# Attention into a squared-ReLU layer: decoding float64 weights with an integer addition of the low word

## The chip, the cores and the metric

The kernel runs on one core of a Trainium2 chip. The metric is device time in microseconds (us), the median of several runs. PE is the matrix engine, DVE the vector engine, ACT the scalar engine (ScalarE), POOL GpSimd, SP the engine that only issues DMAs here. Each engine works through its own list of instructions in order and waits there for what it needs.

## The reference

Eight batches of eight heads, 576 tokens, 64 dimensions a head. Keys and values are first pooled into 32 memory slots by a softmax over tokens (`phi`), then the queries attend to those slots, and the result, as 4608 rows of 512, goes through two weight matrices with a squared ReLU between them.

```python
a = softmax(phi, over tokens)                 # 576 x 32 per head
k_m = einsum('bhsm,bhsd->bhmd', a, k)
v_m = einsum('bhsm,bhsd->bhmd', a, v)
attn = softmax(q @ k_m.T / 8)                 # 576 x 32
x = (attn @ v_m) as (4608, 512)
out = (relu(x @ w_in) ** 2) @ w_out           # w_in 512 x 2048, w_out 2048 x 512
```

`w_in` and `w_out` arrive as float64, everything else as float32.

## The kernel before, in words

Weights are kept as pairs of float32r numbers, a high part and the rest, and each product of two such pairs is made of three matmuls (`hi*hi`, `hi*lo`, `lo*hi`). `v_m @ w_in` is formed first (`vw`), so that the layer's input matrix is small; `mm1` multiplies it with the attention weights (`ath`, `atl`), ScalarE and DVE square the positive part (`r`, `gh`, `glo`), and `mm2` multiplies with `w_out` (`wo`) into four accumulators.

Work runs in this order: the memory slots and attention of batch 0 (`memory`, `scores`, `attention`), then eight steps over slices of `w_in` and blocks of `w_out`, in which weights are decoded just ahead of their first use, batch 1 between them, then pairs of batches with all weights present (`w_out` in SBUF, the decoded `w_in` stored to DRAM in two tensors and read back).

`decode` turns one 128 x 512 piece of float64 into the pair; there are 16 pieces of `w_in` and 16 of `w_out`. A float64 is two 32-bit words: `high` (sign, exponent, 20 bits of mantissa) and `low` (32 bits). They alternate in the buffer `raw`, so that each is read with a step of two words. `work` holds two halves, `T` and `W`. The steps, with lines of the profile:

- L322 (DVE) clamps `high`, read as a float32, to what float32 can hold; L323 (ACT) scales it, which moves the exponent to float32's bias.
- L324 (DVE) takes the sign bit, L325 (DVE) shifts the scaled word left by 3 and joins the sign: `W` now is the weight as float32 with 3 bits of mantissa still zero.
- L326 (DVE) masks `W` down to sign and exponent, a power of two; L327 (DVE) multiplies `low` by 2^-52 and by that power: the value that the low word is worth.
- L330 (DVE) adds the two floats. For the 14 pieces of `w_out` after the first block this addition is left out; a DMA from POOL's queue (L343) adds the value into the lower part of the pair later.
- L338 copies the high part (ACT or DVE, the compiler's helper line is L260), L339 (DVE) subtracts it to get the rest. For `w_in` two DMAs from POOL's queue (L346) store the pair to DRAM.

The kernel records every operation first, with a cost and a latency, and a list planner (`Plan.order`) sets the order in which they are issued; operations that may run on two engines are given to one there. Raw loads, decode and the preparation of later batches are marked as leading work. The framework below may order instructions anew within an engine. So a change of one step's cost moves other steps.

Of the kernel before, what the change touches and what calls it, by code (L numbers as in the profile page):

```python
# [14 lines left out]
AF = mybir.ActivationFunctionType  # L15
ALU = mybir.AluOpType
# [3 lines left out]
P = 128  # L20
EPS = 1e-9
SIGN = 0x80000000
POWER = 0xFF800000
TOP = struct.unpack("<f", struct.pack("<I", 0x47EFFFFF))[0]

STEP = 5200
# [26 lines left out]
class Plan:  # L53
# [21 lines left out]
    def op(self, ways, fn, r=(), w=(), lead=False, cap=None, port=None, size=0, lat=120):  # L75
        o = Op()
        o.ways, o.fn, o.lead, o.cap, o.port, o.size, o.lat = ways, fn, lead, cap, port or {}, size, lat
        deps = set()
        for accesses, writing in ((r, False), (w, True)):
            for a in accesses:  # L80
                b, key = a if isinstance(a, tuple) else (a, None)
                assert not b.closed, b.slot
                if b.before is not None:
                    deps.update(b.before.users)
                for k, ops in b.written.items():
                    if key is None or k is None or k == key:
                        deps.update(ops)
                if writing:
                    for k, ops in b.read.items():
                        if key is None or k is None or k == key:  # L90
                            deps.update(ops)
        for accesses, writing in ((r, False), (w, True)):
            for a in accesses:
                b, key = a if isinstance(a, tuple) else (a, None)
                b.users.append(o)
                if writing:
                    if key is None:
                        b.written, b.read = {None: [o]}, {}
                    else:
                        b.written[key] = [o]  # L100
                        b.read.pop(key, None)
                else:
                    b.read.setdefault(key, []).append(o)
        deps.discard(o)
        o.deps, o.users, o.seq = deps, [], len(self.ops)
        for d in deps:
            d.users.append(o)
        self.ops.append(o)
        return o
# [77 lines left out]
def tt(n):  # L187
    return 150 + 1.04 * n


def ts(n):
    return 150 + 0.52 * n


def act(n):
    return 120 + 0.86 * n
# [10 lines left out]
def tile_attention_moe(  # L207
# [20 lines left out]
    nc = tc.nc  # L228
# [15 lines left out]
    ND = 512  # L244
# [5 lines left out]
    op = plan.op  # L250
    ENG = {"DVE": nc.vector, "POOL": nc.gpsimd, "ACT": nc.scalar}

    def st(shape, dt, tag, name, n=1):
        return plan.buf(tag, lambda slot: sb.tile(shape, dt, tag=slot, name=name, bufs=1), n)
# [4 lines left out]
    def copy(e, o, i):  # L259
        nc.scalar.copy(o, i) if e == "ACT" else ENG[e].tensor_copy(o, i)  # L260

    def dma(fn, size, r=(), w=(), eng="SP", two=False, **more):
        e = {"SP": nc.sync, "POOL": nc.gpsimd}[eng]
        issue = 700 if eng == "POOL" else 1250 if two else 620
        return op({eng: issue}, lambda _: fn(e.dma_start), r=r, w=w, size=size, lat=0, **more)

    def vec(ways, fn, r, w, port=BOTH, **more):
        return op(ways, fn, r=r, w=w, port=port, **more)
# [30 lines left out]
    wo = {}  # L299

    def wi_rows(x, s, hh):

        return w_in_parts[x]()[2 * hh * P:(2 * hh + 2) * P, s * SL:(s + 1) * SL].rearrange("(c p) f -> p c f", p=P)

    def decode(kind, j, h, room):

        rb, wb = (st([P, 2 * ND], U32, tag, name, 2 if tag == "KV" else 1) for tag, name in zip(room, ("raw", "work")))
        if kind == "wi":
            src = w_in_u[:, 2 * h:2 * h + 2, j * SL:(j + 1) * SL, :]
        else:  # L310
            src = w_out_u[:, 2 * j + h:2 * j + h + 1]
        R = rb
        T = lambda: wb()[:, 0:ND]
        W = lambda: wb()[:, ND:2 * ND]
        low = lambda: R().rearrange("p (n t) -> p n t", t=2)[:, :, 0]
        high = lambda: R().rearrange("p (n t) -> p n t", t=2)[:, :, 1]
        tf = lambda: T().bitcast(F32)
        wf = lambda: W().bitcast(F32)
        rk, tk, wk = (rb, "r"), (wb, "t"), (wb, "w")
        dma(lambda d: d(R().rearrange("p (c f t) -> p c f t", c=src.shape[1], t=2), src), 4096 * P, w=[rk], lead=True)  # L320

        vec({"DVE": ts(ND)}, lambda e: nc.vector.tensor_scalar(tf(), high().bitcast(F32), TOP, -TOP, ALU.min, ALU.max), [rk], [tk], lead=True)  # L322
        op({"ACT": act(ND)}, lambda e: nc.scalar.activation(tf(), tf(), AF.Copy, scale=2.0 ** -112), [tk], [tk], lead=True)  # L323
        vec({"DVE": ts(ND)}, lambda e: nc.vector.tensor_scalar(W(), high(), SIGN, None, ALU.bitwise_and), [rk], [wk], lead=True)  # L324
        vec({"DVE": tt(ND)}, lambda e: nc.vector.scalar_tensor_tensor(W(), T(), 3, W(), ALU.logical_shift_left, ALU.bitwise_or), [tk, wk], [wk], lead=True)  # L325
        vec({"DVE": ts(ND)}, lambda e: nc.vector.tensor_scalar(T(), W(), POWER, None, ALU.bitwise_and), [wk], [tk], lead=True)  # L326
        vec({"DVE": tt(ND)}, lambda e: nc.vector.scalar_tensor_tensor(tf(), low(), 2.0 ** -52, tf(), ALU.mult, ALU.mult), [rk, tk], [tk], lead=True)  # L327
        late = kind == "wo" and j > 0
        if not late:
            vec({"DVE": tt(ND)}, lambda e: nc.vector.tensor_add(wf(), wf(), tf()), [tk, wk], [wk], lead=True)  # L330
        if kind == "wi":
            t = wi[0, j, 0, h] = st([P, 2, 2, SL], F32R, "wi", f"wi0_{j}_{h}", 3)
            part = lambda x: t()[:, x].rearrange("p c f -> p (c f)")
        else:
            t = wo[2 * j + h] = st([P, 2, DM], F32R, f"W{j}{'ab'[h]}", f"wo{j}{h}")
            part = lambda x: t()[:, x]
        k0, k1 = ((t, (h, x) if kind == "wi" else x) for x in (0, 1))
        op({"ACT": act(ND), "DVE": ts(ND)}, lambda e: copy(e, part(0), wf()), [wk], [k0], lead=True, port={"DVE": True})  # L338
        vec({"DVE": tt(ND)}, lambda e: nc.vector.tensor_sub(part(1), wf(), part(0).bitcast(F32)),  # L339
            [wk, k0], [k1], lead=True)  # L340
        if late:

            dma(lambda d: d(out=part(1), in_=tf(), accum_op=ALU.add), 4096 * P, [tk, k1], [k1], eng="POOL", lead=True)  # L343
        if kind == "wi":
            for x in (0, 1):
                dma(lambda d, x=x: d(wi_rows(x, j, h), t()[:, x].bitcast(F32)), 2048 * P, r=[(t, (h, x))], w=[(w_in_parts[x], (j, h))], eng="POOL", lead=True)  # L346
# [230 lines left out]
    part = {}  # L577
# [128 lines left out]
    def piece(kind, j):  # L706
        raws, works = (x.split() for x in free[j if j > 3 else 0])
        for h in (0, 1):
            t = turn[0]
            turn[0] += 1  # L710
            decode(kind, j, h, (raws[t % len(raws)], works[t % len(works)]))
# [82 lines left out]
```

## Time and profile before

| | |
|---|---|
| time, median of 3 runs | 836.11 us (831.14 to 837.33) |
| span of the profiled execution | 831.4 us; its own time is not given apart |
| PE busy | 763.5 us (92%) |
| DVE busy | 571.2 us (69%) |
| ACT busy | 378.1 us (45%) |
| DMA | 101.56 MB, mean 122 GB/s |

A busy share is a mean over very different stretches: DVE is near full while weights are decoded and half idle later. The page's lists of waits and the chain of waits tell which engine another one stood still for. The span is the time from the first to the last instruction.

### The profile page before, as it was taken

The numbers are of one execution on the slowest core, as the hardware profiler recorded it, in microseconds if no ns is written. First come the engines' busy times: TensorE is split into PE (matmuls) and PEld (weight loads), VectorE is DVE, ScalarE is ACT, GpSimd is POOL, SyncE is SP. The second block draws the span as 40 slices with busy tenths as digits, with TensorE's granted clock in tenths as the row PEclk, the third lists the DMA queues.
The fourth block names the chain that finished last, engine by engine and source line by source line (L and its number), as shares of the span: only waits on it lengthen the run. The fifth ranks groups of instructions, "written<-read, shape, count | busy, mean of one in ns | idle before, by whom it ended". The sixth has DMA issues, their size and how long they took to land.

```text
span 831.4 us, 12939 instructions
## 1 busy us (share of the span) xinstructions
PE 763.5 (92%) x4756; PEld 643.3 (77%) x4756; DVE 571.2 (69%) x1266; ACT 378.1 (45%) x871; POOL 67.4 (8%) x105
## 2 busy tenths in 40 slices
PE   3468789989989899999999999999999999999995
PEld 2245578878768688888888888888788888888884
DVE  3899899898446756696768465786768556774540
ACT  1235466656535245563436355463435355552320
POOL 3113112222100100001000100000000100000000
PEclk9959999999999899999999999999999999999998
DMA  7947966657665443322552533323422433100001
GB/s 210 302 153 223 261 192 203 178 174 212 159 161 151 116 132 102 102 80 52 143 142 72 135 111 99 117 54 81 140 61 69 138 93 99 53 16 36 1 1 63
DMA packets 93091, 101.56 MB, mean 122 GB/s; under 512 B 24868, under 2 KB 78116, under 8 KB 93028
## 3 DMA queue, kind: packets, MB, share of 16 engines
q1 hardware_dynamic: 80292, 81.55, 33.2%
q0 software_dynamic: 12736, 19.19, 9.5%
q8 instruction: 37, 0.61, 0.3%
q14 instruction: 26, 0.21, 0.1%
HBM read 79.17 MB, written 17.83 MB: 117 GB/s over the span
## 4 chain that ended last, share of the span: by engine, by line
PE 73%; issue 10%; DVE 8%; DMA 3%; ACT 2%; POOL 2%; SPq 0%; POOLq 0%; DVEq 0%; ACTq 0%
PE h L603 20%; PE acc L636 12%; PE acc L633 12%; PE acc L634 12%; PE accl L659 4%; PE pvw L494 4%; PE psc L532 3%; PE pkv L408 3%; DMA q<-in_q_dram 2%; PE pvw L475 1%; DVE vw L503 1%; DVE qT L527 1%; ACT vw L260 1%; DMA wo<-work 1%; DVE work L325 1%
## 5 line engine op out<-in xcount | busy, mean ns | idle before, releaser
L603 PE MATMUL h<-ath,vw 128*128 128x320 f32 (+1 forms) x1024 | 213.9, 300 | 8.9 <-ACT ath L260 6.3
L633 PE MATMUL acc<-wo,gh 128*128 128x512 f32 x512 | 207.0, 404 | 2.7 <-ACT gh L609 2.5
L634 PE MATMUL acc<-wo,gh 128*128 128x512 f32 x512 | 201.7, 394 | 0.0
L603 PEld LDWEIGHTS h<-ath,vw 128*128 128x128 f32 x1024 | 172.5, 190 | 25.7 <-ACT ath L260 6.7
L636 PE MATMUL acc<-wo,glo 128*128 128x512 f32 x512 | 161.5, 409 | 3.0 <-DVE glo L613 2.8
L503 DVE TENSOR_TENSOR vw<-pvw,vw 64x256 fp32r<-64x256 f32 x192 | 78.5, 420 | 68.0 <-ACT vw L260 66.2
L633 PEld LDWEIGHTS acc<-wo,gh 128*128 128x128 f32 x512 | 97.1, 190 | 23.3 <-ACT gh L609 3.8
L260 ACT CAST vw<-pvw 64x256 fp32r<-64x256 f32 (+1 forms) x206 | 74.9, 381 | 83.9 <-PE pvw L494 37.6
L603 PE MATMUL h<-atl,vw 128*128 128x256 f32 (+1 forms) x512 | 110.5, 297 | 0.0
L634 PEld LDWEIGHTS acc<-wo,gh 128*128 128x128 f32 x512 | 96.9, 189 | 16.9
L636 PEld LDWEIGHTS acc<-wo,glo 128*128 128x128 f32 x512 | 90.5, 191 | 21.4 <-DVE glo L613 7.6
L609 ACT ACTIVATE gh<-r 128x512 fp32r<-128x512 f32 x128 | 80.7, 631 | 45.3 <-DVE r L608 38.5
L613 DVE TENSOR_TENSOR glo<-r,gh 128x512 fp32r<-128x512 f32 x128 | 87.6, 684 | 5.1 <-ACT r L611 2.9
L608 DVE TENSOR_SCALAR r<-h 128x256 f32<-128x256 f32 (+1 forms) x109 | 49.7, 458 | 59.0 <-PE h L603 58.1
L607 ACT ACTIVATE r<-h 128x256 f32<-128x256 f32 (+1 forms) x147 | 58.8, 407 | 67.8 <-PE h L603 59.8
L603 PEld LDWEIGHTS h<-atl,vw 128*128 128x128 f32 x512 | 83.0, 190 | 0.5 <-DVE atl L570 0.2
L611 ACT ACTIVATE r<-r 128x576 f32<-128x576 f32 x93 | 63.7, 685 | 2.1
L610 ACT ACTIVATE gl<-r 128x64 fp32r<-128x64 f32 x128 | 32.7, 256 | 63.2 <-DVE r L608 61.0
L659 PE MATMUL accl<-wo,gl 128*128 128x512 f32 x192 | 53.0, 400 | 0.1
L532 PE MATMUL psc<-qT,kb 128*128 128x256 f32 (+1 forms) x128 | 43.3, 465 | 5.8 <-DVE S L536 3.1
L494 PE MATMUL pvw<-wi,VTh 128*128 128x256 f32 x192 | 38.1, 290 | 3.8 <-DVE vw L503 3.7
L659 PEld LDWEIGHTS accl<-wo,gl 128*128 128x128 f32 x192 | 35.4, 191 | 7.3 <-DVE o L260 0.5
(94 smaller groups left out, 818.5 us busy)
## 6 DMA issues: line engine op xcount, KB each, us to landing
wi<-w_in_hi SPq DMA_DIRECT2D x56, 256.0 KB
wi<-w_in_lo SPq DMA_DIRECT2D x56, 256.0 KB
q<-in_q_dram SPq DMA_DIRECT2D x32, 288.0 KB
KV<-in_k_dram SPq DMA_DIRECT2D x32, 256.0 KB
KV<-in_v_dram SPq DMA_DIRECT2D x32, 256.0 KB
raw<-in_moe_w_in_dram SPq DMA_DIRECT2D x16, 512.0 KB
raw<-in_moe_w_out_dram SPq DMA_DIRECT2D x16, 512.0 KB
out_dram<-o POOLq DMA_DIRECT2D x20, 256.0 KB, 8.4
```

What stands on the lines that cost most here:

```text
L260: nc.scalar.copy(o, i) if e == "ACT" else ENG[e].tensor_copy(o, i)
L494: nc.tensor.matmul(pw()[:, x * SL:(x + 1) * SL], l()[:, 2 * hh + x, :], w(r, x), start=(i == 0), stop=(i == 2))
L503: vec({"DVE": tt(SL)}, lambda e, V=V, pr=pr, src=src: nc.vector.tensor_sub(V()[pr, 1, hh, :], src(), V()[pr, 0, hh, :].bitcast(F32)), [pw, ...
L532: nc.tensor.matmul(pq()[:, 0:32 * n], kb()[:, x].rearrange("p h m -> p (h m)"), qT()[:, x, 0:n].rearrange("p c t -> p (c t)"), start=(x == ...
L603: nc.tensor.matmul(p()[:, 0:n], V()[:, l, hh, c0:c0 + P], x()[:, hh, cs], start=(i == 0), stop=(i == 5))
L609: op({"ACT": act(SM)}, lambda e: nc.scalar.activation(gh(), r()[:, 0:SM], AF.Square), [r], [gh])
L611: op({"ACT": act(S), **({} if b < 2 else {"DVE": tt(S)})}, lambda e: nc.scalar.activation(r(), r(), AF.Square) if e == "ACT" else nc.vecto ...
L613: vec({"DVE": tt(SM)}, lambda e: nc.vector.tensor_sub(glo(), r()[:, 0:SM], gh().bitcast(F32)), [r, gh], [glo])
L633: nc.tensor.matmul(a(), gh()[:, c], t()[:, 0], start=f0, stop=False)
L634: nc.tensor.matmul(a(), gh()[:, c], t()[:, 1], start=False, stop=False)
L636: nc.tensor.matmul(a(), glo()[:, c], t()[:, 0], start=False, stop=f1)
L659: nc.tensor.matmul(a(), G()[:, l, :], t()[:, w], start=(ff == 0 and n == 0), stop=(ff == NFF - 1 and n == 2))
```

## The change

The low word is no longer turned into a float. ScalarE multiplies it by 2^-29 and writes it back as a rounded integer (0 to 8) in its place in `raw`; one integer addition on DVE puts it into the three free bits of `W`, with carry. The mask, the product and the float addition go, and so do the 14 accumulating DMAs, for `w_out` pieces are now complete like those of `w_in`.

```diff
-POWER = 0xFF800000
...
         vec({"DVE": tt(ND)}, lambda e: nc.vector.scalar_tensor_tensor(W(), T(), 3, W(), ALU.logical_shift_left, ALU.bitwise_or), [tk, wk], [wk], lead=True)
-        vec({"DVE": ts(ND)}, lambda e: nc.vector.tensor_scalar(T(), W(), POWER, None, ALU.bitwise_and), [wk], [tk], lead=True)
-        vec({"DVE": tt(ND)}, lambda e: nc.vector.scalar_tensor_tensor(tf(), low(), 2.0 ** -52, tf(), ALU.mult, ALU.mult), [rk, tk], [tk], lead=True)
-        late = kind == "wo" and j > 0
-        if not late:
-            vec({"DVE": tt(ND)}, lambda e: nc.vector.tensor_add(wf(), wf(), tf()), [tk, wk], [wk], lead=True)
+        op({"ACT": act(ND)}, lambda e: nc.scalar.activation(low(), low(), AF.Copy, scale=2.0 ** -29), [rk], [rk], lead=True)
+        vec({"DVE": tt(ND)}, lambda e: nc.vector.tensor_tensor(W(), W(), low(), ALU.add), [rk, wk], [wk], lead=True)
...
-        if late:
-
-            dma(lambda d: d(out=part(1), in_=tf(), accum_op=ALU.add), 4096 * P, [tk, k1], [k1], eng="POOL", lead=True)
```

In the changed kernel lines stand one lower up to the new ScalarE line (L325) and the integer addition (L326), and seven lower behind `decode`: the clamp is L321, ACT's scaling L322, the sign L323, the shift L324, the subtraction L335.

The order of the built programs, at three places. First DVE, up to the transpose `at_1_0` of batch 0 (L566, then L559), from the sum `rz_1` of the second head group on. Before:

```order
L397 TENSOR_TENSOR phi_0_170<-phi_0_170,pmx_0_399 128x640
L548 TENSOR_REDUCE rz_1_None<-S_1_384 128x18
L326 TENSOR_SCALAR work<-work 128x512
L549 TENSOR_SCALAR rz_1_None<-rz_1_None 128x18
L322 TENSOR_SCALAR work<-raw 128x512
L550 RECIPROCAL rz_1_None<-rz_1_None 128x18
L327 SCALAR_TENSOR_TENSOR work<-raw,work 128x512
L551 TENSOR_TENSOR S_1_384<-S_1_384,rz_1_None 128x576
L330 TENSOR_TENSOR work<-work 128x512
L566 STREAM_TRANSPOSE at_1_0_445<-S_1_384 128x256
```

Now:

```order
L541 TENSOR_REDUCE rz_1_None<-S_1_409 128x18
L476 TENSOR_TENSOR vw_0_1_473<-pvw_1_0_394,vw_0_1_473 128x512
L542 TENSOR_SCALAR rz_1_None<-rz_1_None 128x18
L326 ISA work<-raw,work 128x1024
L543 RECIPROCAL rz_1_None<-rz_1_None 128x18
L384 TENSOR_REDUCE mx_1_508<-phi_1_273 128x128
L544 TENSOR_TENSOR S_1_409<-S_1_409,rz_1_None 128x576
L426 TENSOR_SCALAR rs_0_517<-pkv_0_452 128x1
L323 TENSOR_SCALAR work<-raw 128x512
L559 STREAM_TRANSPOSE at_1_0_502<-S_1_409 128x256
L427 RECIPROCAL rs_0_517<-rs_0_517 128x1
L324 SCALAR_TENSOR_TENSOR work<-work 128x512
```

The two decode steps L327 and L330 are gone there, and the new addition is one row (`ISA`) over twice the elements. Ahead of the same transpose now stand a subtraction for `vw_0_1`, the next batch's reduction `mx_1` and its `rs_0`, which reads `pkv_0` from PE.

Second ACT, from the cast of the first `vw` on. Before:

```order
L260 CAST vw_0_0_354<-pvw_0_0_329 128x512
L547 ACTIVATE S_0_310<-S_0_310 128x576
L323 ACTIVATE work<-work 128x512 x2
L260 CAST ath_368<-at_0_0_364 128x256
L260 CAST wo_395<-work 128x512
L323 ACTIVATE work<-work 128x512
L547 ACTIVATE S_1_384<-S_1_384 128x576
```

Now:

```order
L259 CAST vw_0_0_332<-pvw_0_0_314 128x512
L259 CAST wo_346<-work 128x512
L325 ACTIVATE raw<-raw 128x512
L322 ACTIVATE work<-work 128x512
L540 ACTIVATE S_0_334<-S_0_334 128x576
L325 ACTIVATE raw<-raw 128x512 x2
L259 CAST wo_365<-work 128x512
L322 ACTIVATE work<-work 128x512
L259 CAST ath_376<-at_0_0_372 128x256
L325 ACTIVATE raw<-raw 128x512
L322 ACTIVATE work<-work 128x512
L325 ACTIVATE raw<-raw 128x512
```

The new row L325 stands ahead of each scaling copy, twice in a row at one place, and the casts of `wo` and `ath` follow behind it.

Third POOL, from the stores of the second slice's pieces to those of the fourth. Before:

```order
L346 DMA w_in_lo<-wi_1_1_518 128x2x256
L343 DMA wo_533<-work 128x512
L343 DMA wo_604<-work 128x512
L346 DMA w_in_hi<-wi_2_0_691 128x2x256
L379 MEMSET phi_1_733 64x4x32
L346 DMA w_in_lo<-wi_2_0_691 128x2x256
L346 DMA w_in_hi<-wi_2_1_729 128x2x256
L346 DMA w_in_lo<-wi_2_1_729 128x2x256
L343 DMA wo_726<-work 128x512
L343 DMA wo_776<-work 128x512
```

Now:

```order
L339 DMA w_in_lo<-wi_1_1_429 128x2x256
L372 MEMSET phi_0_514 64x4x32
L339 DMA w_in_hi<-wi_2_0_693 128x2x256
L339 DMA w_in_hi<-wi_2_1_695 128x2x256
L339 DMA w_in_lo<-wi_2_0_693 128x2x256
L339 DMA w_in_lo<-wi_2_1_695 128x2x256
L372 MEMSET phi_1_709 64x4x32
```

The accumulating DMAs into `wo` are gone; the stores of `w_in` parts follow one another directly.

## Rows read from the trace of the kernel before

**Rows 1.** the page's part 4: the chain that ended last, by engine
```profile
PE 73%; issue 10%; DVE 8%; DMA 3%; ACT 2%; POOL 2%; SPq 0%; POOLq 0%; DVEq 0%; ACTq 0%
```
**Rows 2.** busy time by stretch; columns: stretch, us, engines' busy us (count), PEclk, DMA
```profile
20.00:57.00 37.00, 19.55 (x168) 12.19 (x163) 33.27 (x72) 9.92 (x19) 3.46 (x5) 0.75 0.72 225
57.00:114.00 57.00, 44.25 (x283) 33.94 (x275) 52.94 (x118) 28.15 (x62) 14.37 (x20) 0.92 0.86 248
114.00:209.00 95.00, 90.23 (x534) 79.73 (x534) 84.02 (x176) 60.19 (x132) 19.74 (x25) 1.00 0.63 182
209.00:300.00 91.00, 83.11 (x550) 67.72 (x549) 55.18 (x123) 37.55 (x91) 6.96 (x13) 0.94 0.58 149
300.00:831.00 531.00, 520.32 (x3124) 446.00 (x3122) 339.14 (x764) 238.99 (x564) 15.30 (x28) 0.99 0.29 83
```
**Rows 3.** timeline of DVE; columns: start us, duration us, instruction, [idle before]
```profile
24.70 0.68 DVE L327 SCALAR_TENSOR_TENSOR work<-raw,work 128x512 f32<-128x512 uint32 x1
25.30 0.68 DVE L325 SCALAR_TENSOR_TENSOR work<-work 128x512 uint32<-128x512 uint32 x1
...
56.65 0.44 DVE L566 STREAM_TRANSPOSE at<-S 128x256 f32<-128x256 f32 x1
...
113.65 0.62 DVE L613 TENSOR_TENSOR glo<-r,gh 128x512 fp32r<-128x512 f32 x1
...
208.94 0.69 DVE L613 TENSOR_TENSOR glo<-r,gh 128x512 fp32r<-128x512 f32 x1 [1.67 <-ACT r L611]
```
**Rows 4.** waits of PE in 57:114; columns: total us, times, longest us
```profile
PE acc L636 <- DVE glo L613: 2.4, 3, 1.1
PE acc L633 <- ACT gh L609: 1.5, 1, 1.5
...
PE h L603 <- ACT r L607: 1.2, 2, 0.8
```
**Rows 5.** PE's busy time and granted clock in 46:57
```profile
46.00:57.00 11.00, 6.43 (x87) 0.50 0.39 110
```
**Rows 6.** groups of DVE in 20:209; columns: instruction, count | busy us, mean ns
```profile
L327 DVE SCALAR_TENSOR_TENSOR work<-raw,work 128x512 f32<-128x512 uint32 x32 | 21.8, 681 | 0.1
...
L326 DVE TENSOR_SCALAR work<-work 128x512 uint32<-128x512 uint32 x32 | 13.5, 426 | 0.1
...
L330 DVE TENSOR_TENSOR work<-work 128x512 f32<-128x512 f32 x18 | 12.3, 683 | 0.1
...
L391 DVE TENSOR_REDUCE mx<-phi 128x128 f32<-128x640 f32 x4 | 5.1, 1286 | 0.0
...
L545 DVE TENSOR_TENSOR S<-S,red_None 128x576 f32<-128x576 f32 x4 | 3.0, 749 | 0.0
...
L260 DVE CAST vw<-pvw 128x512 fp32r<-128x512 f32 x2 | 1.4, 682 | 0.0
```
**Rows 7.** timeline of PE: the `pkv` matmuls of batch 1
```profile
54.85 2.52 PE L408 MATMUL pkv<-KV,phi 128*32 128x128 f32 x40
```
**Rows 8.** waits of DVE in 20:209
```profile
DVE work L322 <- DMA wo<-work: 3.1, 2, 1.6
...
DVE work L322 <- DMA raw<-in_moe_w_out_dram: 2.6, 2, 2.4
...
DVE work L322 <- DMA raw<-in_moe_w_in_dram: 2.0, 2, 1.6
```
**Rows 9.** groups of ScalarE (ACT) in 20:209
```profile
L323 ACT ACTIVATE work<-work 128x512 f32<-128x512 f32 x32 | 20.1, 627 | 21.5 <-DVE work L322 21.5
L611 ACT ACTIVATE r<-r 128x576 f32<-128x576 f32 x22 | 15.0, 684 | 0.3
```
**Rows 10.** DMA queues (packets, MB, share of 16 engines) and one issue
```profile
q0 software_dynamic: 12736, 19.19, 9.5%
...
wo<-work POOLq DMA_DIRECT2D x14, 256.0 KB, 5.1
```
**Rows 11.** chain of waits in 265:290; columns: start us, us, what
```profile
272.54 9.02 DMA q<-in_q_dram
```

## Prediction

> **What bounds the kernel now.** First the chain of waits: PE holds most of it [rows 1], so time is won only where PE stands still. Then the stretches [rows 2], cut at three events on the vector engine (DVE) [rows 3]: the first transpose of the second head group of batch 0 (`at_1_0`, 56.65), the fifth `glo` (113.65) and the 22nd (208.94, when the last weight has just been decoded). PE is busy 19.55 of 37 us in 20:57, 44.25 of 57 in 57:114, 90.23 of 95 in 114:209 and 520.32 of 531 after 300 [rows 2]. DVE is busy 33.27 of 37 and 52.94 of 57 in the first two: there it is the bound, and decode is interleaved with attention on it. In 114:209 both are near full. The waits of PE in 57:114 are many and short, the largest sum 2.4 us, on `glo` of DVE [rows 4]: no single wait holds it, the pace of DVE does. [...]
>
> **What the change removes and adds on DVE.** Per piece (32 of 128 x 512) go L326 (426 ns) and L327 (681 ns), and on 18 of them the float add L330 (683 ns); one integer add comes [rows 6]. Neighbours overlap: from L327's start to the next it takes 0.60 us [rows 3], 0.08 less than its mean, so I count each at its mean less 0.08. Removed: 32 x 0.34 + 32 x 0.60 + 18 x 0.60 = 40.9 us.
>
> The price of the new add is the unknown. The order shows it as an `ISA` row over 128x1024: the words as 16-bit halves, twice the elements. Below, it costs a 512-element two-input row, 0.68 us. Above, one half per step: L545 at 576 elements takes 749 ns, L330 at 512 takes 683 [rows 6], so 1.03 ns an element and 1024 of them 1.21 us. L327 is nearest: it reads the same every-other words beside a second input, at 681, the same as contiguous L330. I take 0.83, a quarter of the way up, step 0.75. 32 x 0.75 = 24.0: net 40.9 - 24.0 = 16.9 us less on DVE; with the ends (steps 0.60 and 1.13) 21.7 and 4.7 less.
>
> [...] No row shows a 2-byte operand.
>
> **What the scheduler does with it.** I added the DVE steps along the two built orders up to each event:
> - Up to `at_1_0`: one clamp, two sign masks and one shift-or more, 6 power masks, 6 multiplies and 4 float adds fewer, 7 integer adds more (7 x 0.75); beside them one more `mx` reduction (1286 ns [rows 6], 1.2), two `wi` and one `wo` subtraction and one `vw` subtraction more (0.60 each), one cast (0.34), one small scalar op (0.08). Sum +2.85 us: decode is pulled ahead of batch 0's attention.
> - From there to the fifth `glo`: 2 clamps, 3 sign masks, 2 shift-ors, 10 power masks, 10 multiplies, 6 adds fewer, 8 integer adds more; one `mx`, one `vw`, two `wi`, two `wo` fewer, four casts more. -13.2 us of some 53.
> - From there to the 22nd `glo`: three more of the first kinds (1.3), 16 + 16 + 8 removed ones (-19.8), 17 integer adds (+12.8), and seven casts or copies net that ScalarE did before, two of `vw` and one of `part` at 0.60 (682 ns [rows 6]), the others, from SBUF to SBUF, at a mask's 0.34, with a `wo` subtraction and a transpose: -1.1 us. The casts take back most of what decode gives up here.
>
> **What of it reaches the end.** 20:57: the order also puts `rs` of batch 1, which waits for PE's `pkv`, ahead of `at_1_0`; I price that wait at 1.0 us, between none and the 2.52 us of `pkv` at the low clock [rows 7]. So +2.85 + 1.0 = +3.8, and PE's backlog starts that much later. 57:114: DVE falls to some 40 us, so PE is the bound; at the 0.95 that PE reaches in 114:209 (90.23 of 95 [rows 2]) its 44.25 us take 46.6, that is -10.4. 114:209: PE idles 4.8 us; DVE's 3.1 us of waits for the accumulating DMA [rows 8] go with that DMA, and 1.1 us of work; I credit 1.0, between 0 and 4.8. After 209 nothing: the same work, later waits move along with it. Sum +3.8 - 10.4 - 1.0 = **-7.6 us**. The page gives the span, 831.4, and no time of its own for that execution; the sum makes the span 823.8. The three runs have a median of 836.11, 4.7 over the span; I take the same 7.6 off it: **828.5 us**.
>
> **What lies beside other work.** ScalarE gains 32 `L325`. The nearest row is L323, 627 ns; L611 at 576 takes 684 [rows 9], so if both words of each pair had to pass, 1024 elements would take 1.08 us at 0.89 ns each. I take 0.63: 20 us more, less the casts that go to DVE. It is busy 60.19 of 95 and 28.15 of 57 us [rows 2], which hides them; with the upper end 35 us come into some 90 idle ones of 20:209, still hidden if no one waits. In the built order the new row waits for the load of `raw` alone and stands ahead of the scaling copy; behind it in line are casts, `Relu` and squares, for which PE waits. On POOL 14 accumulating DMAs (`wo<-work`, 256 KB) go [rows 10]; the stores of `w_in` behind them issue sooner, and `wi` is read back from those. They are 3.7 of the 19.19 MB that took queue 0 9.5% of the 16 engines' span, an estimate of 15 us of DMA share; DMA is at 0.86 in 57:114 [rows 2, 10], so I price this at nothing. SP's order has the same loads, some of `raw` earlier; DVE waited for them 4.6 us in all [rows 8].
>
> **Rivals.**
> 1. *The gain stays off the path.* For it: the casts moved to DVE, and ScalarE now waits in line for `raw`: if the 4.6 us that DVE waited for loads [rows 8] come back as waits of PE behind ScalarE, -7.6 + 4.6 = -3.0: 833. Against: DMA carries less, and the loads stand earlier in SP's order.
> 2. *The integer add pays for reading every other word.* [...] Against: L327 reads that stride at 681, contiguous L330 takes 683 [rows 6]. [...]
> 3. *The integer add is dear: DVE stays the bound.* One half per step (step 1.13): +2.7 more up to `at_1_0` (7 x 0.38), nothing in 57:114 (40 + 3 is still under 46.6), +6.5 (17 x 0.38) in 114:209, where DVE has no slack: -7.6 + 9.2 = +1.6, 838. Since no row shows the instruction I allow twice my value too, 1.6 us, step 1.52: 7 x 0.77 + 17 x 0.77 = +18.5 and -7.6 = +10.9, 847. It turns the sign at a step of about 1.07 and costs over 1% from about 1.42. Against: L327's 681 on the same words. For: twice the elements.
> 4. *More than the sum.* Freed DVE also shortens later stalls: PE idles 7.9 us in 209:300, part of it behind a 9.02 us wait for `q` [rows 2, 11], and the early low clock ends sooner. -7.6 - 6 = 822.5.
> 5. *The change doesn't do what it says.* Excluded: the `wo<-work` rows are gone from POOL's order and the 32 `ISA` rows stand in DVE's.
>
> **How the numbers follow.** A median differs from no change, as far as this kernel's runs (0.7% apart) can tell, at about 1%: 8.4 us, 827.7 and 844.5. Forecast 0.44, spread 824 to 831 (the start's wait between 0 and 2.5, the credit between 0 and 4.8): half of it, 0.22, lies under 827.7. Rival 1: 0.20, same. Rival 2: 0.06, same. Rival 3: 0.12, of it 0.06 over 844.5. Rival 4: 0.16, faster. A reordering that goes wrong at a place I don't see: 0.02, slower. Faster 0.22 + 0.16 = 0.38; slower 0.06 + 0.02 = 0.08; within 1% 0.22 + 0.20 + 0.06 + 0.06 = 0.54. The range takes in the forecast, rivals 1 and 2, the milder half of rival 3 and most of rival 4: 818 to 840.
>
> **What would show it.** [...] The forecast is wrong if PE's idle time between `at_1_0` and the fifth `glo` stays near 13 us, or if PE comes to wait for `r` or `gh` of ScalarE by more than the 2.7 us of now [rows 4].

## The result, and the profile after

The changed kernel takes **824.0 us** (median of 4 runs, 820.9 to 825.7), the kernel before beside it 834.6: ratio 0.987, interval 0.983 to 0.991. The profiled run of the changed kernel has a span of 823.3 against 831.4.

The page's engine line, its row of DMA queue 0 and its chain after, to be read against [rows 1, 10]: PE holds 75% of the chain; queue 0 moves 15.52 MB instead of 19.19.

```profile
PE 762.1 (93%) x4756; PEld 643.4 (78%) x4756; DVE 554.3 (67%) x1224; ACT 393.3 (48%) x895; POOL 54.6 (7%) x91
...
q0 software_dynamic: 10720, 15.52, 7.1%
...
PE 75%; DMA 8%; DVE 5%; ACT 4%; SPq 3%; issue 3%; POOL 0%; DVEq 0%; ACTq 0%; POOLq 0%
```

Decode's groups in 20:209 of the changed kernel (instruction, count | busy us, mean ns | idle before it and its releasers), against [rows 6, 9]. The integer add, an `ISA` row in the built order, is L326: 677 ns. The new ScalarE row L325 takes 679 ns, and waits 17.7 us for `raw`.

```profile
L325 ACT ACTIVATE raw<-raw 128x512 uint32<-128x512 uint32 x32 | 21.7, 679 | 17.9 <-DMA raw<-in_moe_w_out_dram 10.1 <-DMA raw<-in_moe_w_in_dram 7.6
...
L326 DVE CUSTOM_DVE_ANT_0 work<-raw,work 128x1024 uint16<-128x1024 uint16 x32 | 21.6, 677 | 0.1
L322 ACT ACTIVATE work<-work 128x512 f32<-128x512 f32 x32 | 19.9, 626 | 4.7 <-DVE work L321 4.4
```

The three events on DVE's timeline, against [rows 3]: `at_1_0` comes 2.15 us later, the fifth `glo` 12.8 us earlier, the 22nd 12.1 us earlier, the end 8.1 us earlier. So some 4 us are given back after the 22nd `glo`: of them 2.0 are PE's work, done later, and 2.0 are idle time.

```profile
58.80 0.42 DVE L559 STREAM_TRANSPOSE at<-S 128x256 f32<-128x256 f32 x1
...
100.87 0.69 DVE L606 TENSOR_TENSOR glo<-r,gh 128x512 fp32r<-128x512 f32 x1 [0.73 <-ACT r L604]
...
196.82 0.69 DVE L606 TENSOR_TENSOR glo<-r,gh 128x512 fp32r<-128x512 f32 x1 [0.19 <-ACT r L604]
```

Such events move when PE's work is shared out otherwise between them. The stretch from `at_1_0` to the fifth `glo`, for one, holds 36.41 us of PE's work, where before it held 44.25 (windows view, columns as in [rows 2]):

```profile
58.80:100.87 42.07, 36.41 (x249) 29.36 (x250) 38.37 (x89) 27.03 (x59) 6.01 (x9) 0.91 0.75 241
```

A plainer account is PE's idle time, stretch less busy time, in fixed stretches. The same view as [rows 2], cut at 20, 60, 100, 200 and 300 (PE, PEld, DVE, ACT and POOL busy with counts, PE's granted clock, DMA share, GB/s), first of the kernel before, then of the changed one:

```profile
20.00:60.00 40.00, 22.00 (x176) 14.01 (x172) 36.27 (x79) 11.85 (x23) 4.38 (x7) 0.74 0.73 228
60.00:100.00 40.00, 30.67 (x209) 23.53 (x210) 35.94 (x82) 19.79 (x46) 9.91 (x13) 0.91 0.85 236
100.00:200.00 100.00, 92.39 (x540) 80.45 (x539) 93.58 (x198) 63.56 (x139) 22.42 (x29) 1.00 0.66 198
200.00:300.00 100.00, 92.07 (x604) 75.58 (x603) 59.61 (x130) 40.63 (x97) 7.81 (x14) 0.95 0.59 150
```

```profile
20.00:60.00 40.00, 21.57 (x173) 14.83 (x174) 35.93 (x77) 19.35 (x36) 6.42 (x10) 0.72 0.83 256
60.00:100.00 40.00, 35.25 (x246) 28.20 (x246) 37.03 (x84) 25.49 (x55) 6.01 (x9) 0.93 0.75 242
100.00:200.00 100.00, 96.72 (x588) 84.73 (x588) 83.70 (x175) 68.45 (x144) 12.32 (x17) 0.97 0.58 179
200.00:300.00 100.00, 91.29 (x581) 76.38 (x580) 60.76 (x136) 42.97 (x104) 7.48 (x13) 0.95 0.51 130
```

PE idles 9.3 us in 60:100 before and 4.8 after, 7.6 and 3.3 in 100:200, 7.9 and 8.7 in 200:300. The first 60 us are alike (31.9 and 32.2), after 300 it is 11.1 and 12.3, and its busy time falls by 1.5. That is the 8.1 us. DVE and the DMA engines both have room that they did not have: DVE's busy time in 100:200 falls from 93.6 to 83.7, the DMA share in 60:100 from 0.85 to 0.75.

The longest wait that is left in the changed kernel stands in 200:300. The chain of waits there (start us, us, what):

```profile
213.70 0.83 DVE phi L390
214.53 0.79 SPq L352
215.37 11.66 DMA phi<-in_phi_dram
227.15 1.23 DVE mx L384
```

and PE's waits in 200:300 (total us, times, longest), first before, then now:

```profile
PE pvw L494 <- DVE vw L503: 3.4, 1, 3.4
PE pkv L408 <- DMA KV<-in_v_dram: 3.0, 1, 3.0
PE pvt L445 <- DVE vx L441: 1.3, 1, 1.3
```

```profile
PE pvt L438 <- DVE vx L434: 8.5, 1, 8.5
```

`vx` of batch 3 stands behind the next head group's `mx` on DVE, `mx` waits for a load of `phi` that takes 11.66 us, and PE waits 8.5 us for `vx`, to start the transpose `pvt`. PE's clock falls with it (same view, PE alone):

```profile
215.00:220.00 5.00, 5.00 (x64) 1.00 0.67 119
220.00:225.00 5.00, 1.68 (x10) 1.00 0.81 186
225.00:230.00 5.00, 0.00 (x0) 0.56 0.74 217
230.00:235.00 5.00, 4.78 (x14) 0.50 0.27 70
235.00:240.00 5.00, 5.00 (x34) 0.92 0.00 2
```

### The profile page after: what moved, and what is told of

Read it like the earlier page. It is cut to its first block, busy times and chain, and to the rows that moved or that the text cites. A ratio compares the mean times of both kernels' runs of the same rounds, so it can differ in the third digit from the quotient of the medians.

```text
span 823.3 us, 12864 instructions
## 1 busy us (share of the span) xinstructions
PE 762.1 (93%) x4756; PEld 643.4 (78%) x4756; DVE 554.3 (67%) x1224; ACT 393.3 (48%) x895; POOL 54.6 (7%) x91
## 3 DMA queue, kind: packets, MB, share of 16 engines
q0 software_dynamic: 10720, 15.52, 7.1%
## 4 chain that ended last, share of the span: by engine, by line
PE 75%; DMA 8%; DVE 5%; ACT 4%; SPq 3%; issue 3%; POOL 0%; DVEq 0%; ACTq 0%; POOLq 0%
PE h L596 21%; PE acc L626 13%; PE acc L629 13%; PE acc L627 12%; PE accl L652 5%; PE pvw L487 4%; PE psc L525 3%; DMA phi<-in_phi_dram 2%; DMA raw<-in_moe_w_out_dram 2%; PE pkv L401 2%; DMA raw<-in_moe_w_in_dram 2%; PE pvw L468 2%; SPq L353 1%; SPq L352 1%; ACT vw L259 1%
## 5 line engine op out<-in xcount | busy, mean ns | idle before, releaser
L596 PEld LDWEIGHTS h<-ath,vw 128*128 128x128 f32 x1024 | 173.0, 192 | 29.0 <-ACT ath L259 11.3
L596 PE MATMUL h<-atl,vw 128*128 128x320 f32 (+1 forms) x512 | 111.2, 299 | 0.0
L602 ACT ACTIVATE gh<-r 128x512 fp32r<-128x512 f32 x128 | 80.7, 630 | 35.8 <-DVE r L601 31.4
L601 DVE TENSOR_SCALAR r<-h 128x320 f32<-128x320 f32 (+1 forms) x110 | 50.2, 459 | 59.7 <-PE h L596 59.1
L596 PEld LDWEIGHTS h<-atl,vw 128*128 128x128 f32 x512 | 83.7, 192 | 0.4
L604 ACT ACTIVATE r<-r 128x576 f32<-128x576 f32 x98 | 67.1, 684 | 2.3
L525 PE MATMUL psc<-qT,kb 128*128 128x256 f32 (+1 forms) x128 | 40.7, 440 | 3.9 <-DVE S L529 2.3
```

Source lines behind the costliest of these rows:

```text
L525: nc.tensor.matmul(pq()[:, 0:32 * n], kb()[:, x].rearrange("p h m -> p (h m)"), qT()[:, x, 0:n].rearrange("p c t -> p (c t)"), start=(x == ...
L596: nc.tensor.matmul(p()[:, 0:n], V()[:, l, hh, c0:c0 + P], x()[:, hh, cs], start=(i == 0), stop=(i == 5))
L602: op({"ACT": act(SM)}, lambda e: nc.scalar.activation(gh(), r()[:, 0:SM], AF.Square), [r], [gh])
L604: op({"ACT": act(S), **({} if b < 2 else {"DVE": tt(S)})}, lambda e: nc.scalar.activation(r(), r(), AF.Square) if e == "ACT" else nc.vecto ...
```

## The experiments

The theory was that the gain is DVE work taken out of the stretches that DVE paces. The rivals: the accumulating DMAs that are gone, the new order, and, against the gain, ScalarE's new instruction. The table has PE's idle time in stretches of the one profiled run of each kernel (stretch less busy time, us), with the medians of all runs and their ratios to the kernel before, each taken beside it:

| kernel | median | ratio, interval | 20:60 | 60:100 | 100:200 | 200:300 | 300 to end |
|---|---|---|---|---|---|---|---|
| before | 834 | 1 | 18.0 | 9.3 | 7.6 | 7.9 | 11.1 |
| changed | 824.0 | 0.987 (0.983 to 0.991) | 18.4 | 4.8 | 3.3 | 8.7 | 12.3 |
| dead_one | 840.5 | 1.007 (1.005 to 1.010) | 18.6 | 10.2 | 6.5 | 11.3 | 11.6 |
| dead_two | 849.4 | 1.018 (1.015 to 1.022) | 21.4 | 8.6 | 9.0 | 8.9 | 11.8 |
| ghost | 822.3 | 0.986 (0.982 to 0.989) | 17.8 | 6.2 | 5.4 | 7.9 | 11.9 |
| dead_dma | 832.0 | 0.997 (0.995 to 1.000) | 19.8 | 4.2 | 8.4 | 8.9 | 13.2 |
| dma_ghost | 823.6 | 0.988 (0.985 to 0.990) | 18.3 | 3.3 | 3.8 | 10.8 | 11.7 |
| dma_tiny | 824.1 | 0.989 (0.986 to 0.991) | 18.8 | 4.4 | 2.8 | 9.1 | 12.1 |
| no_acc | 832.9 | 0.999 (0.997 to 1.002) | 18.3 | 8.7 | 6.9 | 4.2 | 12.4 |
| phi_lat | 823.8 | 0.987 (0.984 to 0.990) | 17.1 | 5.4 | 3.5 | 8.7 | 11.8 |
| late_store | 823.5 | 0.988 (0.985 to 0.990) | 17.8 | 4.3 | 2.4 | 9.2 | 12.4 |
| shift_or | 817.5 | 0.980 (0.977 to 0.983) | 20.0 | 3.5 | 4.5 | 4.4 | 12.1 |
| shift_or_store | 818.5 | 0.982 (0.979 to 0.984) | 17.6 | 3.6 | 1.8 | 4.8 | 12.5 |
| so_same_order | 821.5 | 0.983 (0.980 to 0.986) | 19.3 | 4.4 | 0.8 | 9.2 | 12.2 |

**DVE's work put back, without the DMAs.**

```diff
-        vec({"DVE": tt(ND)}, lambda e: nc.vector.tensor_tensor(W(), W(), low(), ALU.add), [rk, wk], [wk], lead=True)
+        def add(e):
+            nc.vector.scalar_tensor_tensor(tf(), low(), 2.0 ** -52, tf(), ALU.mult, ALU.mult)
+            nc.vector.tensor_tensor(W(), W(), low(), ALU.add)
+
+        vec({"DVE": tt(ND)}, add, [rk, wk], [wk, tk], lead=True)
```

> The changed kernel with one dead multiply (the removed L327, its result unused) issued right before each of the 32 integer adds, the order of everything else unchanged. Its step is 0.60 us, so DVE's decode per piece is 1.20 us against 1.28 in the kernel before and 0.60 in the changed one; no accumulating DMA comes back. Theory (the gain is DVE work taken out of the stretches that DVE paces): 7 adds ahead of at_1_0 cost +4.2 us, the 9 up to the fifth glo +1.7 to +5.4 (DVE is busy 38.4 of 42.1 us there), the 17 up to the 22nd about half of their 10.2; sum +11, so about 835, between 831 and 838. Rival (the gain is the DMAs that are gone, or the order): 822 to 827.

dead_two has the dead multiply twice.

> The same with two dead multiplies per integer add: 64 steps of 0.60 us. Theory (DVE work): every further step counts in full once DVE has no slack, +24 us or so against the changed kernel, 843 to 852. Rival (DMAs or order): still 822 to 830.

840.5, 2.5 us over its range, and 849.4, within it. DVE's work counts, nearly in full at first: 32 x 0.60 = 19.2 us of it cost 16.5 us, the next 19.2 another 8.9. So dead_two came out in its range, but not for the reason given, that every further step counts in full; why the second half cost less is open. In 60:100 of dead_one PE has lost its clock as well, 0.75 where it was 0.93 (the windows view):

```profile
60.00:100.00 40.00, 29.84 (x210) 22.99 (x203) 31.48 (x72) 19.48 (x45) 3.29 (x6) 0.75 0.58 176
```

DVE's total busy time in dead_one (571.6 us) is that of the kernel before (571.2), with less DMA, yet it is 0.7% slower. What costs the rest is open. One candidate is the order: it was planned for less work on DVE, and it is not quite that of the changed kernel, as was expected, for the edit writes `T` too and many neighbours on DVE change places; the last integer add starts at 212.37 us, in the changed kernel at 183.66. Another is the ScalarE instruction, which waits 29.6 us for `raw` there and 17.7 in the changed kernel. So 16.5 us is more than DVE's work alone has to cost; no_acc below gives a second measure.

**The order alone.** The removed mask and multiply planned, not issued:

```diff
+        vec({"DVE": ts(ND)}, lambda e: None, [wk], [tk], lead=True)
+        vec({"DVE": tt(ND)}, lambda e: None, [rk, tk], [tk], lead=True)
         op({"ACT": act(ND)}, lambda e: nc.scalar.activation(low(), low(), ...
```

> The changed kernel, but the scheduler still plans the removed mask and multiply at their old durations (nothing is issued for them), so its order stays near that of the kernel before while DVE's work is that of the changed one. Theory (work removed counts, the order is secondary): the gain stays, 818 to 828, and at_1_0 comes no later than 57 us. Rival (the gain is the new order): 830 to 835.

822.3, and `at_1_0` at 55.12: the gain does not need the new order, nor the later `at_1_0` that comes with it.

**The DMAs put back, without DVE's work.**

```diff
+        if kind == "wo" and j > 0:
+            dma(lambda d: d(out=T(), in_=W(), accum_op=ALU.add), 4096 * P, [wk, tk], [tk], eng="POOL", lead=True)
```

> The changed kernel with 14 accumulating DMAs of 256 KB put back on POOL, at the places of the old ones, from one half of the work tile to the dead other half; no matmul waits for them. Theory (DVE work): 822 to 827, no change beside the changed kernel. Rival (the traffic that is gone made the gain): 828 to 833. If the DMA's hold on the work tile stalls DVE (3.1 us in the kernel before), up to +3.

The rival holds: 832.0. Nothing waits for what these DMAs write except the next clamp on the same work tile, and they take back nearly all of the gain. Two runs in nearly the same order part the reasons, one that issues none and one that moves 8 of 512 columns:

```diff
-            dma(lambda d: d(out=T(), in_=W(), accum_op=ALU.add), ...
+            dma(lambda d: None, ...
+            dma(lambda d: d(out=T()[:, 0:8], in_=W()[:, 0:8], accum_op=ALU.add), ...
```

> The order of the run dead_dma, whose 14 DMAs brought the time to 832.0, but the DMAs are planned only: none is issued. If the 8 us come from what the DMAs do (their traffic, or the work tile they hold): 822 to 827. If they come from the order that the scheduler makes when it reckons with them: 830 to 833.

> The order of dead_dma once more, with its 14 DMAs cut to 8 of 512 columns: each still reads the work tile after the integer add and holds it until it has landed, but moves a 64th of the bytes. If the traffic costs the 8 us: 822 to 827, near dma_ghost. If the hold on the work tile does, through the next clamp that waits for it: 828 to 832. If the order does: 830 to 833 as dma_ghost.

823.6 and 824.1: neither the order, nor 14 more issues on POOL, nor the hold of a short DMA on the work tile costs anything that the runs show. It is the full transfers, 3.67 MB: their bytes on the DMA engines, or the longer hold on the work tile that comes with them (median 5.9 us from issue to landing, 3.9 in dma_tiny). The page's row of queue 0 (packets, MB, share), the windows view of 100:200 and PE's waits in 60:200, of dead_dma:

```profile
q0 software_dynamic: 12736, 19.19, 9.4%
```

```profile
100.00:200.00 100.00, 91.57 (x519) 79.88 (x518) 81.45 (x166) 65.74 (x140) 19.85 (x25) 0.97 0.66 188
```

```profile
PE acc L628 <- ACT gh L604: 3.7, 3, 2.0
PE h L598 <- ACT r L602: 3.6, 6, 1.8
PE pvw L470 <- DVE vw L478: 2.0, 2, 1.1
```

The same three of dma_tiny:

```profile
q0 software_dynamic: 12736, 15.58, 7.4%
```

```profile
100.00:200.00 100.00, 97.21 (x564) 85.49 (x564) 84.05 (x171) 67.04 (x144) 20.34 (x26) 0.98 0.57 180
```

```profile
PE acc L628 <- ACT gh L604: 2.0, 2, 1.5
...
PE h L598 <- ACT r L602: 0.9, 4, 0.3
PE pvw L470 <- DVE vw L478: 0.4, 1, 0.4
```

With the bytes, the DMA share of 100:200 is 0.66, without them 0.57, and PE idles 8.4 us instead of 2.8. None of PE's waits in 100:200 is on a DMA: they are on `gh`, `r` and `vw`, each of an engine that also decodes (9.3 us in the three rows of 60:200 against 3.3; in 100:204 alone 8.4 against 2.6). In 100:204 ScalarE waits 10.0 us for `raw` with the bytes and 7.8 without, DVE 3.9 and 1.5 us for the accumulating DMA itself. Which of these two passes the delay on, later loads or the hold on the work tile, was not tried apart.

**The reverse.** The kernel before without its accumulating DMAs, the float add on DVE in every piece:

```diff
-        late = kind == "wo" and j > 0
+        late = False
```

> The kernel before with the float add on DVE in all 32 pieces: the 14 accumulating DMAs go, and DVE gets 14 adds of 0.60 us. Theory (DVE work alone decides): 8.4 us more of it in the paced stretches, 836 to 842. Rival (the DMAs cost as much as dead_dma showed, 8 us): the two cancel, 826 to 834.

832.9, no change: the 14 adds cost what the 14 DMAs cost. That fits a kernel that stands at both limits: moving work from one to the other gains nothing. Beside the changed kernel this run is also the fairer price of DVE's work. Neither has the accumulating DMAs, each has an order planned for its own work, DVE is busy 579.4 us against 554.3, and the time is 8.9 us longer (ScalarE has 32 instructions fewer in no_acc).

**The stall of `pvt`.** It is PE's wait for `vx` above, from 222 to 230 us; the expectations name it by the issue of the `phi` load, near 215 us. Two edits aimed at that load. phi_lat has the scheduler issue it earlier:

```diff
-        dma(lambda d: tokens(d, a(), phi[b, 4 * hh:4 * hh + 4]), 4 * S * M * 4, [], [(A, "in")], two=True, lead=True)
+        dma(lambda d: tokens(d, a(), phi[b, 4 * hh:4 * hh + 4]), 4 * S * M * 4, [], [(A, "in")], two=True, lead=True, lat=6000)
...
-                o.end = wire + LANDS[e]
+                o.end = wire + LANDS[e] + o.lat
```

> The changed kernel with the scheduler told that a load of phi lands 6 us later than it thought; in the built order SP issues the phi load that ended the 8.5 us stall of pvt near 215 us directly after the first KV load instead of behind all eight. If that load's place in the queue makes the stall: phi lands 3 to 5 us earlier and the time falls by as much, 818 to 822. If it is DMA bandwidth that is short there: the wait moves to KV loads and the time stays, 822 to 826.

823.8. SP issues this `phi` load at 209.99 us instead of 213.93, and the wait moves from `phi` to `KV`, as the second theory has it (PE's waits after 197 us):

```profile
PE pkv L401 <- DMA KV<-in_v_dram: 8.6, 1, 8.6
```

So it is not the place of that one load. late_store was to take the output stores of batch 1 out of that place:

```diff
+            def put(r=(), store=store):
+                dma(store, 32 * n * DM * 4, [home, *r], [], eng="SP" if b >= B - 2 else "POOL")
+
+            if b == 1 and n == 4:
+                held.append(put)
...
         for b in (b0, b1):
             for hh in (0, 1):
                 memory(b, hh)
+        while held:
+            held.pop(0)([newest[0]])
```

> The changed kernel with the four output stores of batch 1 (L678 on POOL, issued between 213 and 217 us, 11.4 us to land) made to wait for the last vx of batches 2 and 3. If their writes slow the phi and KV loads that they run beside and so make the 8.5 us stall of pvt: the stall shrinks to 1 to 3 us and the time falls to 816 to 820. If the loads are slow by themselves: the stall stays near 8 us, 822 to 826.

823.5, but this run shows nothing about the stores, for they did not move. `vx` stands in the planner's list of reads alone; in the built program nothing makes POOL wait for it. The timeline of POOL, first of the changed kernel, then of late_store:

```profile
213.37 1.44 POOL L678 DMA_DIRECT2D out_dram<-o  x2 [4.49 <-ACT o L259]
215.64 1.37 POOL L678 DMA_DIRECT2D out_dram<-o  x2 [0.83 <-DVE o L259]
```

```profile
210.77 1.44 POOL L682 DMA_DIRECT2D out_dram<-o  x2 [4.48 <-ACT o L259]
213.04 1.37 POOL L682 DMA_DIRECT2D out_dram<-o  x2 [0.83 <-DVE o L259]
```

The last `vx` of batches 2 and 3, which they should have followed, starts at 239.69 us. All comes 2.6 us earlier, the load of `phi` too, and it takes as long (chain of late_store):

```profile
211.93 0.80 SPq L352
212.77 12.10 DMA phi<-in_phi_dram
224.98 1.23 DVE mx L387
```

So late_store is the changed kernel once more, and whether the stores slow the loads of `KV` and `phi` stays open. They could: in 208:232 of the changed kernel they are on queue 0, the loads on queue 1 (packets, MB, share of the 16 engines):

```profile
q1 hardware_dynamic: 4780, 2.93, 43.4%
q0 software_dynamic: 1088, 1.05, 24.0%
```

**ScalarE's part.** The low word goes in by one shift-or on DVE (truncated, not rounded), and the 32 L325 go:

```diff
-        op({"ACT": act(ND)}, lambda e: nc.scalar.activation(low(), low(), AF.Copy, scale=2.0 ** -29), [rk], [rk], lead=True)
-        ... nc.vector.tensor_tensor(W(), W(), low(), ALU.add) ...
+        ... nc.vector.scalar_tensor_tensor(W(), low(), 29, W(), ALU.logical_shift_right, ALU.bitwise_or) ...
```

> The changed kernel without ScalarE's rounding: DVE shifts the low word right by 29 and ors it into the work word in one instruction (the weight is truncated to float32, not rounded), so the 32 L325 go and DVE keeps one two-input step per piece, near 0.68 us. If ScalarE's 21.7 us beside PE and DVE are covered: 822 to 825. If its wait in line for raw (17.9 us in the changed kernel) holds back Relu and squares: 817 to 821.

> Both edits, the late stores and the shift-or. If both mechanisms hold and do not overlap: 812 to 817. If only the stores count: as late_store.

817.5 is **the best version here, 2.0% under the kernel before**. shift_or_store (818.5, intervals overlap) misses its 812 to 817, but the stores have not moved in it either (POOL issues them at 210.81 to 213.94 us), so it all but repeats shift_or. The time of shift_or lies where ScalarE's wait for `raw` was to be the cause, but the gain stands in the wrong place for it: in 20:200 PE idles 27.9 us in shift_or and 26.5 in the changed kernel; it is in 200:300 that 8.7 became 4.4, and PE's busy time is 2.9 us shorter. The last run has the same shift-or and nearly the order of the changed kernel:

```diff
-        op({"ACT": act(ND)}, lambda e: nc.scalar.activation(low(), low(), AF.Copy, scale=2.0 ** -29), [rk], [rk], lead=True)
+        op({"ACT": act(ND)}, lambda e: None, [rk], [rk], lead=True)
...
```

> The shift-or of the run before, but the scheduler still plans the removed ScalarE rounding (nothing is issued for it), so the built order is that of the changed kernel but for a few neighbours that change places. If the 6.5 us that shift_or won beside the changed kernel come from ScalarE's 32 instructions and its wait for raw: 815 to 820 again. If they come from the order, by which the stall of 8.5 us near 215 us was 4.1 there: 822 to 825.

821.5, between the two, its interval touching both. In its profile the stall is back (9.1 us on `vx`), and 100:200 is nearly free of idle time, 0.8 us. PE's waits in 60:200 on ScalarE, first of the changed kernel, then of this run: the one for `gh` is shorter, that for `r` is not.

```profile
PE acc L626 <- ACT gh L602: 2.8, 2, 2.0
...
PE h L596 <- ACT r L600: 1.4, 4, 0.6
```

```profile
PE h L596 <- ACT r L600: 1.5, 4, 0.6
PE acc L626 <- ACT gh L602: 0.6, 1, 0.6
```

So ScalarE's row may cost some 2.5 us in 100:200, and the order of shift_or may save some 4 us later. Neither is shown: each rests on one profile, and late_store, which has the row, idles only 2.4 us in 100:200.

## Why the prediction was right, and where its terms were wrong

The forecast was 828.5 with 818 to 840; 824.0 lies inside, 1.3% under the kernel before, on the edge of the likeliest case and towards rival 4. The sum was near (-7.6 against -8.1 in the spans) partly by luck. In its terms PE's idle time changed by -0.1 up to `at_1_0` (forecast +3.8), -7.1 to the fifth `glo` (-10.4), -1.5 to the 22nd (-1.0) and +2.0 after it (0), and its busy time by -1.5, which the sum does not have: two errors of over 3 us cancel.

- **The bound.** "DVE is the bound" in the first two stretches holds: dead_one brings the work back and loses 16.5 us, and no_acc, with 25.1 us more of it, is 8.9 us slower than the changed kernel. It is one of two causes.
- **The step that failed**: "DMA is at 0.86 in 57:114, so I price this at nothing". Beside the 1.0 us credited in 114:209, partly for DVE's waits for that DMA, the removed transfers stand at nothing in the sum. They are worth about 8 us: dead_dma against dma_tiny, 832.0 and 824.1. In the rows DVE waits 3.1 us for this DMA [rows 8], and PE's longest waits in 57:114 are on DVE and ScalarE [rows 4], so I took the transfers for covered. They cost through waits on other engines (9.3 us in 60:200 for `gh`, `r` and `vw`, against 3.3 in dma_tiny), and mostly in 100:200 (8.4 us of PE's idle time against 2.8), where the share was only 0.66.
- **Both together.** The parts do not add: giving back either the DVE work or the DMAs loses all or nearly all of the gain, and no_acc, which trades the one for the other, moves nothing. My sum credited DVE with nearly all of it.
- **The add's price.** Taken as 0.83 us, measured 0.677, the lower bound. Rivals 2 and 3 fall with it. No run shows a charge for reading every other word, which is rival 2: this row takes 677 ns, L327 on the same words 681 and the contiguous L330 683 [rows 6]. Nor does a run show how the row passes its 16-bit halves; 1024 of them took what 512 floats take.
- **ScalarE.** L325 taken as 0.63, measured 0.679. PE's waits for `r` and `gh` in 60:200 are 4.2 us (before 4.7), so rival 1 did not come; that a cheaper form is worth up to 2.5 us stays open.
- **The stretches.** Start +3.8: `at_1_0` is 2.15 later, but PE's idle time up to it is the same, 31.4 and 31.3 us, so it cost nothing. `at_1_0` to the fifth `glo` -10.4: the stretch shrank by 14.9, of it 7.8 are PE work now done elsewhere (44.25 to 36.41 us) and 7.1 idle time; PE reaches 0.87 there, not 0.95. (The steps listed for this stretch add up to -12.7 at the prices given, not -13.2; the term goes by PE's pace and does not change.) To the 22nd `glo` -1.0: idle time fell 1.5. After it 0: idle time rose 2.0, of it 0.8 in 200:300, where the stall of `pvt` stands. DVE's busy time up to the 22nd `glo` fell by 15.0 us, not the 11.5 of the sums given (+2.85, -13.2, -1.1). The fifth and the 22nd `glo` came 12.8 and 12.1 us earlier, more than the 6.6 and 7.6 that the sum has up to them.
- **Rival 4** said that later stalls would shrink: they did not, one of 8.5 us stands where three of 7.7 in all stood.

## What to carry to other kernels

A transfer that the busiest engine never waits for need not be free: here 14 of them, of 256 KB each, cost 8 us (832.0 against 824.1 in dma_tiny) and came back as waits of PE for the engines that decode, by later loads or by a longer hold on a buffer. Before crediting one resource with a gain, put its work back as dead work, and the other's too; where either alone takes the gain away, both count. Count PE's idle time in fixed stretches, not the shift of events, when a scheduler reorders the work. And look in the trace whether an edit moved what it was to move before reading its time: in late_store it had not, and the unchanged time looked like an answer.

## What the runs showed of the hardware

- The integer add over 1024 16-bit halves takes 677 ns; the 512-element float product and float add of the kernel before take 681 and 683 [rows 6], and the shift-or of the same every-other words 679 in so_same_order.
- ScalarE's scaling of every other 32-bit word, integers in and out, takes 679 ns, of contiguous floats 626.
- 14 accumulating transfers of 256 KB on queue 0, 3.67 MB, cost 8 us of time (dead_dma against dma_tiny); most of it stands in 100:200, where PE idled 8.4 us with them and 2.8 without, at a mean DMA share of 0.66 and 0.57.
- A load of `phi` (288 KB) took 11.66 us in the changed kernel and 12.10 in late_store, both with four stores of 256 KB issued within 3 us of it; the DMA share in the changed kernel was 0.67 to 0.81 meanwhile.
- In the changed kernel PE stood still for 8.5 us in 222 to 230 us; its granted clock was 0.56 in 225:230, 0.50 in 230:235, though it was busy 4.78 of those 5 us, and 0.92 in the next 5 us.
